# Seven half-width products in place of eight: the w_out product of an mLSTM cell with a gated feed-forward block

## The chip, the cores and the metric

The kernel runs on one core of one Trainium2 chip. The metric is the device time of one execution in microseconds; lower is better. All arithmetic is in fp32.

A core has five engines with a queue of instructions each. TensorE (PE in the profile) multiplies matrices and writes to PSUM, an accumulator memory of eight banks. Its weight loads (PEld), which bring in the stationary operand, overlap its matmuls. VectorE (DVE), ScalarE (ACT) and GpSimd (POOL) work element by element; SyncE (SP) issues transfers. GpSimd does not read or write PSUM in this kernel.

## The reference, cut to what matters

```python
# first part: mLSTM cell over B, H, S, D = 4, 8, 768, 40, step by step over t
m_new  = maximum(f[t] + m, i[t])
C      = exp(f[t] + m - m_new) * C + exp(i[t] - m_new) * outer(v[t], k[t])
n      = exp(f[t] + m - m_new) * n + exp(i[t] - m_new) * k[t]
y[t]   = sigmoid(o[t]) * (C @ q[t]) / maximum(abs(n . q[t]), 1)

# second part: x = y as (B*S, H*D) = (3072, 320)
h   = x @ w_in           # w_in: 320 x 2048
g   = h * cos(h)
out = g @ w_out          # w_out: 2048 x 320
```

The change concerns the last line.

## The kernel before, in words

The sequence of 768 tokens is cut into 6 chunks of 128 (`c`). In each, the cell of every batch `b` (4 of them) is computed with matrices over the 128 tokens: scores, a decay matrix `E`, values, a state carried from chunk to chunk, and a normalisation that writes the transposed input `xT[c]` of the second part. The cell of chunk `c + 1` is computed while the second part of chunk `c` runs. The cells of the first chunk come ahead of everything, in `first_cells`, and the last chunk has no cell beside it.

The second part of a chunk works on 512 tokens at once, the 128 of all four batches. The 2048 hidden columns are 16 blocks of 128, taken in pairs; the pair's number is `f2`, 0 to 7, and `e`, 0 or 1, is the block in the pair. For each pair:

- `Up(c, f2)` computes `h` transposed for the two blocks, each 128 x 512, in two PSUM banks (`pup`, L613 and L616).
- `near`, `rest`, `sin` and `gate` compute the gated value: ScalarE finds the nearest whole number of turns (L621), VectorE takes the rest (L624), ScalarE the sine (L629), and VectorE multiplies (L633). The result is `g`, 128 hidden columns by 512 tokens, in SBUF, in a pool of six buffers.
- `down(c, f2)` adds to the four accumulators `po[c]`, one bank for each batch, 128 tokens x 320 columns, over all 16 blocks. The stationary operand of each matmul is the part of `g` that belongs to a batch; the moving operand is a block of `w_out` (L645). So a pair takes 8 matmuls of 320 columns. After the last pair of a chunk each accumulator is copied by ScalarE (L648) and sent out (L649).

The order of all instructions is written out by hand in `first_cells` and `both_parts`, under `manual_schedule`. One call of `both_parts(c, b)` is a step with two half steps, pairs `2 b` and `2 b + 1`. Each begins with an `Up`, and a `down` follows one half step later: the `down` of a pair comes after the next pair's `Up`, so that ScalarE and VectorE compute `g` in between. The last `down` of a chunk therefore lies in the first half step of the next chunk:

```python
        if f2 > 0:
            down(c, f2 - 1)
        elif c > 0:
            down(c - 1, NF // 2 - 1)
```

Between them lie the cell's parts: `scores` (L445) in the first half step after `Up`, then `weigh` (L451, VectorE), `decay_exponents` of the next cell (L370 on VectorE, L371 on GpSimd) and `decay` (L379, the exponential on ScalarE). After `down` come `values_turned` (L482, L488, into the banks `hp`) and `normalize_turned` (L502 to L514, VectorE, which reads `hp`). The second half step has `seam` (L580, matmuls for the state, into banks of the same pool as `hp`), `state` (L596, VectorE), `weigh_k` (L392, GpSimd), and `turn_blocks` (L410 to L417, VectorE) for the next cell. `fade` (L565) scales the state, on GpSimd in chunk 1 and on VectorE later.

PSUM is fully used: two banks for `pup`, two for the cell (pool `ps_a`), four for `po` (pool `ps_o`).

The weights come in as 64-bit numbers. They are staged in SBUF (`bits`), and turned into fp32 by ScalarE, VectorE and GpSimd (`parts` and `join`, L138 to L149) during chunk 0, pair by pair of blocks for `w_out`.

Of the kernel before, what the change touches and what calls it, by code (L numbers as in the profile page):

```python
# [11 lines left out]
FP = mybir.dt.float32  # L12
# [4 lines left out]
OP = mybir.AluOpType  # L17
# [12 lines left out]
def kernel(  # L30
# [20 lines left out]
    nc = tc.nc  # L51

    B, H, S, D = q.shape
    C = 128
    NC = S // C
# [3 lines left out]
    DM = H * D  # L59
    DFF = moe_w_in.shape[1]  # L60
    NF = DFF // 128
# [13 lines left out]
    p2 = ctx.enter_context(tc.tile_pool(name="p2", bufs=2))  # L75
    p3 = ctx.enter_context(tc.tile_pool(name="p3", bufs=3))
    p4 = ctx.enter_context(tc.tile_pool(name="p4", bufs=4))
    pb = ctx.enter_context(tc.tile_pool(name="pb", bufs=5))
    pc = ctx.enter_context(tc.tile_pool(name="pc", bufs=3))
# [3 lines left out]
    ps_o = ctx.enter_context(tc.tile_pool(name="ps_o", bufs=4, space=bass.MemoryType.PSUM))  # L83
# [15 lines left out]
    p1 = ctx.enter_context(tc.tile_pool(name="p1", bufs=1))  # L99
# [20 lines left out]
    w_out_sb = wp.tile([128, NF, DM], FP, name="w_out_sb")  # L120
# [11 lines left out]
    def parts(dst, bits):  # L132
        n = dst.shape[1]
        hi, lo = bits[:, 0:n, 1], bits[:, 0:n, 0].bitcast(U32)
        t = p2.tile([128, WQ], I32, name="wt", tag="wt")[:, 0:n]
        m = p2.tile([128, WQ], I32, name="wm", tag="wm")[:, 0:n]

        nc.scalar.activation(out=t.bitcast(FP), in_=hi.bitcast(FP), func=AF.Abs)  # L138

        nc.scalar.activation(out=m, in_=lo, func=AF.Copy, scale=2.0 ** -29)  # L140
        return dst, hi, t, m

    def join(dst, hi, t, m, last=None):
        nc.vector.tensor_scalar(out=t.bitcast(FP), in0=t.bitcast(FP), scalar1=LEAST, scalar2=GREATEST,
                                op0=OP.max, op1=OP.min)
        nc.vector.tensor_scalar(out=t, in0=t, scalar1=5, scalar2=2, op0=OP.logical_shift_left,
                                op1=OP.logical_shift_right)
        nc.vector.scalar_tensor_tensor(out=t, in0=hi, scalar=TOP2, in1=t, op0=OP.bitwise_and, op1=OP.bitwise_or)
        (last or nc.gpsimd).tensor_tensor(out=dst.bitcast(I32), in0=t, in1=m, op=OP.add)  # L149
# [210 lines left out]
    def psum_o():  # L360
        return ps_o.tile([128, HP, C], FP, name="pm", tag="o")

    def cols(n, j, width):
        c, b = divmod(n, B)
        return tab[:, c, j, ts(b, H)].unsqueeze(2).to_broadcast([128, H, width])
# [23 lines left out]
    def weigh_k(n):  # L389
        if n < N - B:  # L390
            kw = p2.tile([128, H, D], FP, name="kw", tag="kw")
            nc.gpsimd.tensor_tensor(out=kw, in0=ks[n % NB][:, :, 0:D], in1=cols(n, 1, D), op=OP.mult)  # L392
            kws[n] = kw
# [44 lines left out]
    def scores(n):  # L438
        pool, tag = psum(n)
        qT, kT = qkT[n]  # L440
        ps = [pool.tile([128, HP, C], FP, name="ps", tag=tag) for _ in range(2)]
        for p in range(HP):
            for j in range(2):
                r = slice(64 * j, 64 * j + (64 if n < TURNED else D))
                nc.tensor.matmul(ps[j][:, p], kT[r, p], qT[r, p], start=True, stop=True)  # L445
        pss[n] = ps
# [6 lines left out]
    def values_kept(n):  # L453

        pool, tag = (ps_o, "o") if n == B else psum(n)
        heads_of[n] = None
        if n >= B:
            pq = pool.tile([128, H, D1], FP, name="pq", tag=tag)
            for p in range(HP):
                nc.tensor.matmul(pq[:, 2 * p:2 * p + 2].rearrange("p j d -> p (j d)"), qkT[n][0][:, p],  # L460
                                 st[n % B][:, p].rearrange("p j d -> p (j d)"), start=True, stop=True)
            heads_of[n] = pq
# [136 lines left out]
    gs, po = {}, {}  # L599

    class Up:
# [21 lines left out]
        def rest(self, e):  # L623
            nc.vector.scalar_tensor_tensor(out=self.n[e].bitcast(FP), in0=self.pu[e], scalar=0.25, in1=self.n[e],  # L624
                                           op0=OP.add, op1=OP.subtract)
# [5 lines left out]
        def gate(self, e):  # L631
# [2 lines left out]
                                           op0=OP.mult, op1=OP.mult)  # L634
            gs[self.c, 2 * self.f2 + e] = g

    def down(c, f2):
        if f2 == 0:
            po[c] = [ps_o.tile([128, DM], FP, name="po", tag="o") for _ in range(B)]

        order = [(f, b) for f in (2 * f2, 2 * f2 + 1) for b in range(B)]
        if f2 == NF // 2 - 1:
            order.sort(key=lambda fb: fb[1])
        for f, b in order:
            nc.tensor.matmul(po[c][b], gs[c, f][:, ts(b, C)], w_out_sb[:, f], start=(f == 0), stop=(f == NF - 1))  # L645
            if f == NF - 1:
                o = p2.tile([128, DM], FP, name="o_sb", tag="o_sb")
                nc.scalar.copy(out=o, in_=po[c][b])  # L648
                nc.sync.dma_start(out=out[b * S + c * C:b * S + (c + 1) * C], in_=o)  # L649


    pw, pmu = (ps_u.tile([128, HP, C], FP, name=name, tag="up") for name in ("pw", "pmu"))
# [1 line left out]
    def warm(k, bank=None):  # L654

        for _ in range(k):
            nc.tensor.matmul(bank or pw, nil, nil.unsqueeze(1).to_broadcast([128, HP, 128]), start=True, stop=True)
# [131 lines left out]
    def both_parts(c, b):  # L789

        n = (c + 1) * B + b
        cell = n < N
        begin = c == b == 0
        more = cell and n + 1 < N
        f2 = 2 * b
        up = Up(c, f2)
        if cell:  # L800
            scores(n)
            if begin:
                values_kept(n)

                warm(6, psum_o())
        for e in range(2):
            up.near(e)
        if begin:
            weigh(n)
        for e in range(2):  # L810
            up.rest(e)
        if cell and not begin:
            weigh(n)
        if begin or more and c > 0:
            decay_exponents(n + 1)
        for e in range(2):
            up.sin(e)
            up.gate(e)
        if c == 0 and b == 1:
            sigmoid(1, slice(1, B))  # L820
        if b == B - 1 and c + 2 < NC:
            sigmoid(c + 2)
        h = ()
        if begin:
            h = out_parts()
            w = parts(*pieces.pop(0))
        else:
            if c == 0:
                out_join(*out_parts())
            if pieces:  # L830
                join(*parts(*pieces.pop(0)))
        if begin or more and c > 0:
            decay(n + 1)
        elif more:
            decay_by_bias(n + 1)
        if f2 > 0:
            down(c, f2 - 1)
        elif c > 0:
            down(c - 1, NF // 2 - 1)
        if cell:  # L840
            if n + 2 < N:
                load(n + 2)
            if n < TURNED:
                if not begin:
                    values_kept(n)
                values(n)
                normalize(n)
            else:
                values_turned(n)
            if begin:  # L850
                out_join(*h, nc.vector)
            if TURNED <= n + 2 < N:
                load_G(n + 2)
            if n + 3 < N:
                load_E(n + 3)
            if b == B - 2 and c + 2 < NC:
                load_o(c + 2)
            if n >= TURNED:
                normalize_turned(n)
            fade(n)  # L860
        h = w if begin else ()
        if not begin:
            sin_next()
        if pieces and not begin:
            h = parts(*pieces.pop(0))
        up = Up(c, f2 + 1)
        if cell:
            seam(n)
        for e in range(2):
            up.near(e)  # L870
        for e in range(2):
            up.rest(e)
        if cell and n < TURNED:
            seam_out(n)
        if h:
            join(*h)
        if cell:
            state(n)
        for e in range(2):
            up.sin(e)  # L880
            up.gate(e)
        if more:
            weigh_k(n + 1)
        if pieces:
            join(*parts(*pieces.pop(0)))
        down(c, f2)
        if pieces:
            join(*parts(*pieces.pop(0)))
        if c == 0:
            if b + 2 < B:  # L890
                pieces.extend(weights_in(b + 2))
            h = out_parts()
        if more and n + 1 < TURNED:
            turn(n + 1)
            turn_out(n + 1, c > 0)
        elif more:
            turn_blocks(n + 1)
        if c == 0:
            out_join(*h)

    pieces, outs = [], []
    with tc.manual_schedule():
        first_cells()
        for c in range(NC):
            for b in range(B):
                both_parts(c, b)
        down(NC - 1, NF // 2 - 1)


# [28 lines left out]
```

## Time and profile before

| | |
|---|---|
| time, median of 3 runs | 550.35 us (550.14 to 550.5) |
| span in the profile | 549.5 us |
| granted TensorE clock, mean | 0.993 |
| matmuls of L645 (w_out) | 768 records, 219.3 us busy |
| matmuls of L613 and L616 (w_in) | 384 and 192 records, 175.5 and 54.2 us busy |
| chunk 0's second part begins | 38.7 us |
| chunks 1 to 5 begin | 132.6, 217.2, 301.7, 386.2, 469.0 us |
| last `Up` ends, about | 536.6 us |

Busy time is the union of the records' spans, so that overlapping matmuls are not counted twice; the mean duration of one record is longer than the distance to the next. One fp32 matmul of the code gives two records on PE and two on PEld. "Idle before" is the time in which an engine stood still ahead of a group, and the name behind it is what ended the wait.

### The profile page before, as it was taken

Reading aid. Unit: us, or ns where it says so; the run is one execution under the profiler, and the core shown is the slowest. Engines: PE = TensorE matmul, PEld = TensorE weight load, DVE = VectorE, ACT = ScalarE, POOL = GpSimd, SP = SyncE. Lnnn points to the kernel's source line nnn. Section 1 sums busy time; section 2 is a strip of 40 time slices with the busy share of each in tenths; the row PEclk is TensorE's granted clock in tenths of the full one; section 3 lists DMA queues with packets and bytes.
Section 4 is the critical chain, followed back from the end, with each engine's and each line's share of the span. In section 5 each row is a group of like instructions: output and inputs, shape, how many; then the busy total and the mean of one; then the engine's idle time right before and its main releaser. Section 6 shows DMA issues by size and latency. Waiting matters only on the chain.

```text
span 549.5 us, 9153 instructions
## 1 busy us (share of the span) xinstructions
PE 538.8 (98%) x3395; PEld 317.4 (58%) x3395; DVE 355.9 (65%) x692; ACT 264.4 (48%) x420; POOL 76.7 (14%) x112
## 2 busy tenths in 40 slices
PE   9989899999999999999999999999999999999997
PEld 6865566665565565565565555555655655555554
DVE  5876987968777677677667667667666665232311
ACT  4868795775632544543435344427335323331312
POOL 5531433523110100101101101100000000000000
PEclk9979999999999999999999999999999999999999
DMA  9999985851265651166625076635075000100001
GB/s 143 206 226 221 239 220 145 189 124 33 77 142 129 148 124 36 50 136 138 151 75 107 26 158 139 143 78 110 4 173 109 8 14 12 51 1 1 0 0 50
DMA packets 134509, 56.83 MB, mean 103 GB/s; under 512 B 72080, under 2 KB 130528, under 8 KB 134464
## 3 DMA queue, kind: packets, MB, share of 16 engines
q1 hardware_dynamic: 134320, 56.04, 46.0%
q8 instruction: 27, 0.44, 0.3%
q0 software_dynamic: 96, 0.18, 0.2%
q14 instruction: 18, 0.15, 0.1%
q10 hardware_dynamic: 48, 0.02, 0.0%
HBM read 50.00 MB, written 6.21 MB: 102 GB/s over the span
## 4 chain that ended last, share of the span: by engine, by line
PE 85%; DVE 5%; DMA 4%; SPq 3%; POOL 1%; ACT 1%; issue 1%; DVEq 0%; ACTq 0%; POOLq 0%
PE po L645 37%; PE pup L613 28%; PE pup L616 8%; PE hp L488 3%; PE ps L445 3%; PE hp L482 2%; PE pu L580 1%; DMA E<-M_d 1%; SPq L327 1%; PE pt L426 1%; SPq L129 1%; DMA qs<-in_q_dram 1%; DMA bits<-in_moe_w_out_dram 1%; DMA M_d<-M_rows 1%; DMA bits<-in_moe_w_in_dram 1%
## 5 line engine op out<-in xcount | busy, mean ns | idle before, releaser
L645 PE MATMUL po<-w_out_sb,g 128*128 128x320 f32 x768 | 219.3, 439 | 1.3 <-POOL w_out_sb L149 1.0
L645 PEld LDWEIGHTS po<-w_out_sb,g 128*128 128x128 f32 x768 | 142.0, 190 | 67.0 <-issue 8.3
L613 PE MATMUL pup<-xT,w_in_sb 128*128 128x512 f32 x384 | 175.5, 599 | 0.9 <-POOL w_in_sb L149 0.6
L621 ACT ACTIVATE n<-pup 128x512 int32<-128x512 f32 x96 | 52.0, 593 | 214.3 <-PE pup L616 214.3
L624 DVE SCALAR_TENSOR_TENSOR n<-pup,n 128x512 f32<-128x512 f32 x96 | 61.9, 686 | 135.1 <-ACT n L621 135.0
L613 PEld LDWEIGHTS pup<-xT,w_in_sb 128*128 128x128 f32 x384 | 71.2, 191 | 77.6 <-issue 63.9
L629 ACT ACTIVATE n<-n 128x512 f32<-128x512 f32 x96 | 58.8, 630 | 12.1 <-DVE n L624 12.1
L633 DVE SCALAR_TENSOR_TENSOR g<-pup,n 128x512 f32<-128x512 f32 x96 | 61.7, 685 | 1.7
L371 POOL TENSOR_SCALAR_AFFINE_SELECT E<-E 128x1024 f32<-128x1024 f32 x19 | 20.8, 1094 | 292.9 <-DVE E L370 273.6
L616 PE MATMUL pup<-xT,w_in_l 64*128 64x512 f32 x192 | 54.2, 641 | 0.0
L616 PEld LDWEIGHTS pup<-xT,w_in_l 64*128 64x128 f32 x192 | 14.4, 184 | 36.4 <-issue 35.6
L451 DVE TENSOR_TENSOR E<-ps,E 128x512 f32<-128x512 f32 x48 | 30.7, 680 | 6.1 <-PE ps L445 6.1
L379 ACT ACTIVATE E<-E 128x1024 f32<-128x1024 f32 x21 | 22.2, 1058 | 21.7 <-POOL E L371 17.2
L410 DVE STREAM_TRANSPOSE t<-qs 128x512 f32<-128x512 f32 x32 | 32.3, 1087 | 0.0
L445 PEld LDWEIGHTS ps<-t,t 40*128 40x128 f32 (+1 forms) x384 | 25.1, 188 | 9.7 <-issue 8.9
L445 PE MATMUL ps<-t,t 40*128 40x128 f32 (+1 forms) x384 | 25.8, 274 | 0.0
L370 DVE TENSOR_TENSOR E<-E,tab 128x1024 f32<-128x1024 f32 x19 | 23.1, 1216 | 0.4 <-DMA E<-M_d 0.4
L379 ACT ACT_TABLE_LOAD x18 | 23.1, 1283 | 0.3
L778 ACT ACT_TABLE_LOAD x18 | 23.1, 1283 | 0.3
L502 DVE STREAM_TRANSPOSE room<-hp 128x128 f32<-128x128 f32 x32 | 8.6, 306 | 22.5 <-PE hp L488 22.5
L488 PE MATMUL hp<-E,vs 128*32 128x128 f32 x512 | 17.3, 276 | 0.0
L417 DVE STREAM_TRANSPOSE room<-o 128x256 f32<-128x256 f32 x32 | 17.2, 618 | 0.0
(128 smaller groups left out, 428.9 us busy)
## 6 DMA issues: line engine op xcount, KB each, us to landing
E<-M_d SPq DMA_DIRECT2D x22, 512.0 KB
bits<-in_moe_w_in_dram SPq DMA_DIRECT2D x40, 128.0 KB
bits<-in_moe_w_out_dram SPq DMA_DIRECT2D x8, 640.0 KB
room<-G_d SPq DMA_DIRECT2D x32, 128.0 KB
ks<-in_k_dram SPq DMA_DIRECT2D x24, 160.0 KB
vs<-in_v_dram SPq DMA_DIRECT2D x24, 160.0 KB
out_dram<-o_sb SPq DMA_DIRECT2D x24, 160.0 KB
qs<-in_q_dram SPq DMA_DIRECT2D x32, 80.0 KB
```

The source lines that it names most:

```text
L379: nc.scalar.activation(out=Es[n], in_=Es[n], func=AF.Exp, scale=-1.0)
L410: nc.vector.transpose(out=dst.rearrange("r p (t x) -> r p x t", x=T4), in_=src.rearrange("r p (x d) -> r p x d", x=T4)[:, :, :, 0:32])
L445: nc.tensor.matmul(ps[j][:, p], kT[r, p], qT[r, p], start=True, stop=True)
L451: nc.vector.tensor_tensor(out=w, in0=pss[n][j], in1=w, op=OP.mult)
L488: nc.tensor.matmul(hps[n][j][ts(p, 32), half], vs[n % NB][:, h, lo:lo + DA], Es[n][:, h], start=False, stop=True, skip_group_check=True)
L613: nc.tensor.matmul(pu, w_in_sb[:, i, ts(block(f2, e), 128)], x(i), start=(i == 0), stop=False)
L616: nc.tensor.matmul(pu, w_in_l[r, f2], x(NK, r), start=False, stop=True)
L621: nc.scalar.activation(out=self.n[e], in_=self.pu[e], func=AF.Copy, bias=0.25)
L624: nc.vector.scalar_tensor_tensor(out=self.n[e].bitcast(FP), in0=self.pu[e], scalar=0.25, in1=self.n[e], op0=OP.add, op1=OP.subtract)
L629: nc.scalar.activation(out=r, in_=r, func=AF.Sin, scale=TWO_PI_DOWN)
L633: nc.vector.scalar_tensor_tensor(out=g, in0=self.pu[e], scalar=TWO_PI, in1=self.n[e].bitcast(FP), op0=OP.mult, op1=OP.mult)
L645: nc.tensor.matmul(po[c][b], gs[c, f][:, ts(b, C)], w_out_sb[:, f], start=(f == 0), stop=(f == NF - 1))
```

## The change

Write the 128-token parts of `g` for batches 0 and 1 and the two blocks of a pair as a 2 x 2 matrix of blocks, A11 (batch 0, block 0), A21 (batch 1, block 0), A12 and A22, and the two halves of 160 columns of the two blocks of `w_out` as B11, B12 (block 0) and B21, B22 (block 1). The product of two such matrices needs eight block products. Winograd's form of Strassen's algorithm needs seven, with sums formed before and after:

| sums of g (`S`) | differences of w_out (`T`) | products |
|---|---|---|
| S0 = A21 + A22 | T0 = B12 - B11 | P1 = A11 B11, P2 = A12 B21 |
| S1 = S0 - A11 | T1 = B22 - T0 | P3 = S3 B22, P4 = A22 T3 |
| S2 = A11 - A21 | T2 = B22 - B12 | P5 = S0 T0 |
| S3 = A12 - S1 | T3 = T1 - B21 | P6 = S1 T1, P7 = S2 T2 |

The outputs are C11 = P1 + P2, C12 = P1 + P6 + P5 + P3, C21 = P1 + P6 + P7 - P4 and C22 = P1 + P6 + P7 + P5. Each of the seven is summed over the eight pairs in PSUM, so that the last sums are formed once for each chunk.

The change does this for batches 0 and 1 in chunks 1 to 5. Batches 2 and 3, and all of chunk 0, keep their products. The parts:

- GpSimd forms the `T` of a pair once (`two_differences`, in the last half step of chunk 0 and three of chunk 1), in buffers that held the staged weights. It forms the `S` of every pair and chunk after the second `gate` (`sums`).
- The accumulators are grouped by bank: P1, P2, P6 in the first, P5, P3, P4 in the second, batch 2 and P7 in the third, batch 3 in the fourth. Only the first matmul into a bank clears it.
- At a chunk's end ScalarE copies P1, VectorE makes seven additions out of PSUM, and ScalarE copies batches 3 and 2. ScalarE's copies stand behind all writes to their bank. The last `down` of a chunk is now issued ahead of `decay`, and its copies and transfers (`rest`) after it. At the very end of the kernel, the seven products come before the two whole batches.

```diff
+    def differences(p, T):
+        B11, B12, B21, B22 = (w_out_sb[:, 2 * p + e, ts(h, DH)] for e in range(2) for h in range(2))
+        for i, (x, y) in enumerate(((B12, B11), (B22, T[:, 0]), (B22, B12), (T[:, 1], B21))):
+            nc.gpsimd.tensor_tensor(out=T[:, i], in0=x, in1=y, op=OP.subtract)
...
+    def sums(c, f2):
...
+        S = p2.tile([128, 4, C], FP, name="sg", tag="wt")
+        A11, A21, A12, A22 = (gs[c, 2 * f2 + e][:, ts(b, C)] for e in range(2) for b in range(2))
+        for i, (x, y, op) in enumerate(((A21, A22, OP.add), (S[:, 0], A11, OP.subtract),
+                                        (A11, A21, OP.subtract), (A12, S[:, 1], OP.subtract))):
+            nc.gpsimd.tensor_tensor(out=S[:, i], in0=x, in1=y, op=op)
...
+    def down_parted(c, f2):
...
+            po[c] = [ps_o.tile([128, 3 * DH + 32], FP, name="po", tag="o") for _ in range(4)]
+        P1, P2, P6, P5, P3, P4 = (po[c][i // 3][:, ts(i % 3, DH)] for i in range(6))
+        P7 = po[c][2][:, DM:DM + DH]
...
+        very_end = end and c == NC - 1
+        if not very_end:
+            for b in range(2, B):
+                whole(b)
+        product(P1, g0[:, 0:C], w0[:, lo], True)
+        product(P2, g1[:, 0:C], w1[:, lo])
+        product(P6, S[:, 1], T[:, 1])
+        product(P7, S[:, 2], T[:, 2])
+        product(P5, S[:, 0], T[:, 0], True)
+        product(P3, S[:, 3], w1[:, hi])
+        product(P4, g1[:, C:2 * C], T[:, 3])
...
+        nc.scalar.copy(out=U[:, 0], in_=P1)
+        for dst, x, y, op in ((o2[:, 0, lo], U[:, 0], P2, OP.add), (U[:, 0], U[:, 0], P6, OP.add),
+                              (U[:, 1], U[:, 0], P7, OP.add), (U[:, 0], U[:, 0], P5, OP.add),
+                              (o2[:, 0, hi], U[:, 0], P3, OP.add), (o2[:, 1, lo], U[:, 1], P4, OP.subtract),
+                              (o2[:, 1, hi], U[:, 1], P5, OP.add)):
+            nc.vector.tensor_tensor(out=dst, in0=x, in1=y, op=op)
+        if very_end:
+            for b in (3, 2):
+                whole(b)
...
     def down(c, f2):
+        if parted(c):
+            return down_parted(c, f2)
...
             up.gate(e)
+        sums(c, f2)
...
+        rest = None
+        if b == 0 and c > 0 and parted(c - 1):
+            rest = down(c - 1, NF // 2 - 1)
         if begin or more and c > 0:
             decay(n + 1)
...
+        elif rest:
+            rest()
         elif c > 0:
             down(c - 1, NF // 2 - 1)
...
+        sums(c, f2 + 1)
         if more:
             weigh_k(n + 1)
+        if c == 0 and b == B - 1 or c == 1 and b < B - 1:
+            two_differences(c * (2 * b + 2))
```

In the changed kernel the products of both kinds stand in line 689, the sums of `g` in line 672, the weight differences in line 651, the copy of P1 in line 715 and the seven additions in line 720.

More of the change, by code (lines that the diff above doesn't have):

```diff
@@ L635, in gate, with parted, two_differences @@
             gs[self.c, 2 * self.f2 + e] = g
+    DH = DM // 2
+    Ts, sg = {}, {}
+    def parted(c):
+        return c > 0
+    def differences(p, T):
+        B11, B12, B21, B22 = (w_out_sb[:, 2 * p + e, ts(h, DH)] for e in range(2) for h in range(2))
+        for i, (x, y) in enumerate(((B12, B11), (B22, T[:, 0]), (B22, B12), (T[:, 1], B21))):
+            nc.gpsimd.tensor_tensor(out=T[:, i], in0=x, in1=y, op=OP.subtract)
+        Ts[p] = T
+    def two_differences(p):
+        if p < 6:
+            T = pc.tile([128, 2, 4, DH], FP, name="T", tag="bits")
+            for e in range(2):
+                differences(p + e, T[:, e])
+        else:
+            for e in range(2):
+                differences(p + e, pb.tile([128, 4, DH], FP, name="T", tag="bits"))
@@ new lines, in sums @@
+    def sums(c, f2):
+        if not parted(c):
+            return
+        S = p2.tile([128, 4, C], FP, name="sg", tag="wt")
[3 more added lines that the diff above has]
+            nc.gpsimd.tensor_tensor(out=S[:, i], in0=x, in1=y, op=op)
+        sg[c, f2] = S
@@ new lines, in down_parted, with product, whole, whole_out @@
+    def down_parted(c, f2):
+        end = f2 == NF // 2 - 1
+        if f2 == 0:
+            po[c] = [ps_o.tile([128, 3 * DH + 32], FP, name="po", tag="o") for _ in range(4)]
+        P1, P2, P6, P5, P3, P4 = (po[c][i // 3][:, ts(i % 3, DH)] for i in range(6))
+        P7 = po[c][2][:, DM:DM + DH]
+        g0, g1 = (gs[c, 2 * f2 + e] for e in range(2))
+        w0, w1 = (w_out_sb[:, 2 * f2 + e] for e in range(2))
+        S, T = sg[c, f2], Ts[f2]
+        lo, hi = slice(0, DH), slice(DH, DM)
+        def product(out, g, w, first=False):
+            nc.tensor.matmul(out, g, w, start=(f2 == 0 and first), stop=end, skip_group_check=True)
+        def whole(b):
+            for e, (g, w) in enumerate(((g0, w0), (g1, w1))):
+                product(po[c][b][:, 0:DM], g[:, ts(b, C)], w, e == 0)
+        def whole_out(b):
+            o = p2.tile([128, DM], FP, name="o_sb", tag="o_sb")
+            nc.scalar.copy(out=o, in_=po[c][b][:, 0:DM])
+            result(c, b, o)
+        very_end = end and c == NC - 1
[9 more added lines that the diff above has]
+        product(P4, g1[:, C:2 * C], T[:, 3])
+        if not end:
+            return None
+        o2 = p2.tile([128, 2, DM], FP, name="o2", tag="wm")
+        U = p1.tile([128, 2, DH], FP, name="hs", tag="hs")
+        nc.scalar.copy(out=U[:, 0], in_=P1)
[7 more added lines that the diff above has]
+                whole(b)
+        def rest():
+            for b in range(2):
+                result(c, b, o2[:, b])
+            for b in (3, 2):
+                whole_out(b)
+        return rest
@@ L637, in down, with result @@
+    def result(c, b, o):
+        nc.sync.dma_start(out=out[b * S + c * C:b * S + (c + 1) * C], in_=o)
     def down(c, f2):
+        if parted(c):
+            return down_parted(c, f2)
         if f2 == 0:
@@ L648, in down @@
                 nc.scalar.copy(out=o, in_=po[c][b])
-                nc.sync.dma_start(out=out[b * S + c * C:b * S + (c + 1) * C], in_=o)
+                result(c, b, o)
     pw, pmu = (ps_u.tile([128, HP, C], FP, name=name, tag="up") for name in ("pw", "pmu"))
@@ L906 @@
                 both_parts(c, b)
-        down(NC - 1, NF // 2 - 1)
+        down(NC - 1, NF // 2 - 1)()
 _INS = ['q', 'k', 'v', 'i_gate', 'f_gate', 'o_gate', 'moe_w_in', 'moe_w_out']
```

## The prediction, made before the changed kernel ran

> **What bounds the kernel now.** I read the page's busy shares first, then the slices by stage, then the chain of work that ended last, then the groups by line with their shapes kept apart, then the timeline around one half step. The first three say the same thing.
>
> ```profile
> PE 538.8 (98%) x3395; PEld 317.4 (58%) x3395; DVE 355.9 (65%) x692; ACT 264.4 (48%) x420; POOL 76.7 (14%) x112
> ...
> PE 85%; DVE 5%; DMA 4%; SPq 3%; POOL 1%; ACT 1%; issue 1%; DVEq 0%; ACTq 0%; POOLq 0%
> ```
>
> ```profile
> 217.20:301.70 84.50, 84.50 (x609) 48.53 (x608) 59.48 (x122) 37.86 (x54) 7.18 (x9) 1.00 0.48 107
> 301.70:386.20 84.50, 84.50 (x609) 48.53 (x608) 59.50 (x121) 37.69 (x54) 6.48 (x8) 1.00 0.47 107
> 386.20:469.00 82.80, 82.80 (x546) 46.99 (x545) 53.09 (x103) 31.56 (x49) 3.28 (x3) 1.00 0.24 54
> 469.00:536.60 67.60, 67.60 (x210) 35.12 (x208) 18.05 (x28) 18.05 (x36) 0.00 (x0) 1.00 0.03 10
> ```
>
> The columns of the second fence are stretch, length, then busy time of PE, PEld, DVE, ACT and POOL, the granted clock and DMA. From 132.6 us, where chunk 1 begins, PE never stops: in chunks 2 to 5 its busy time equals the stretch, and the chain in chunk 2 consists of PE alone. A saved nanosecond of PE is therefore a saved nanosecond of kernel until another engine falls behind. GpSimd is almost idle.
>
> A busy PE is not yet a PE at its limit, so I take the cost of one matmul from its spacing:
>
> ```profile
> 128.23 4.57 PE L645 MATMUL po<-w_out_sb,g 128*128 128x320 f32 x16
> ```
>
> ```profile
> L470 PE MATMUL ph<-vs,E 128*128 128x41 f32 x128 | 15.5, 282 | 0.2 <-DVE E L451 0.2
> L470 PEld LDWEIGHTS ph<-vs,E 128*128 128x128 f32 x128 | 15.0, 192 | 0.7 <-DVE E L451 0.4
> ```
>
> One `down` is 8 matmuls in the code and 16 in the trace, since each fp32 matmul appears as two with a weight load each. Of the 4.57 us the last takes 0.43 and the first costs about 0.10 more than its successors (its start follows another tile shape), so the spacing is (4.57 - 0.43 - 0.10) / 15 = 269 ns, which is also the start-to-start time of the single records. The durations of 439 ns overlap. The rows of L470 give the other limit: its matmuls have 41 columns, so the weight load of 128 columns must set their pace. Loads last 192 ns each but 128 of them cover 15.0 us, 117 ns each with the ends of 8 bursts; start to start the records show 112 ns.
>
> [...]
>
> **The change part by part.**
> *The products.* In chunks 1 to 5, 8 half steps each, two of four batches lose 4 matmuls of 320 columns and get 7 of 160; 40 such exchanges. Removed: 4 x 2 x 269 = 2152 ns. Added: 7 x 2 x the spacing at 160 columns. No row has this width with full 128 x 128 weights. Bounds: the weight-load pace, 112 ns (L470 at 41 columns and L357 at 128 columns both run at it)[...]. The larger must hold; I take 136. The load is hidden with 24 ns to spare. 14 x 135.8 = 1901 ns. Saving 252 ns an exchange, x 40 = 10.1 us.
>
> *Sums on GpSimd* (L672 of the changed kernel, four 128 x 128 operations a half step). Two-input rows: 723 ns for 320 elements (L392), 501 for 164 (L565 on POOL). The line through them gives 450 ns at 128[...]. Four take about 1.8 us, 2.0 at most. They start at the end of the second `gate` and are needed by the third product of a `down` that comes after the next `Up`. In chunk 3, gates end at 311.90 and 322.03, the `down`s that use them start at 318.43 and 328.31, and the third product comes 1.7 us later: 8.0 us or more. The work of PE itself hides them. Behind them in GpSimd's queue stand `weigh_k` (its product is wanted a half step later), the mask L371 of the following step (which waits for VectorE until 331.90), and in chunk 1 `fade`. Only after the last `Up` is there no next one to hide behind; there P6 and P3 may wait some tenths of a us.
>
> *Weight differences on GpSimd*: 32 operations of 160 columns, about 0.5 us each, in four lots of 4 us in chunk 0's last half step and chunk 1's. GpSimd is busy 8.7 of 84.6 us in chunk 1: hidden. They overlap VectorE's L413 (two SBUF inputs, 0.68 us), whose result has 2 us to spare.
>
> *More readers and waits.* A `gate` now also waits for GpSimd's reading of a `g` three `Up`s old; that is long over. From the last gate to the next `Up` there are at least 0.81 us of slack in chunks 1 to 4 (322.03 to 322.84 is the shortest), and the second bank is needed 0.86 later still. The shorter `down` takes 0.25 from it. PE gets three satisfied GpSimd waits a half step. L470 has two such waits a burst and keeps its 112 ns, so I cost them at nothing; the other end is 50 ns each (the length of a wait record on PEld) less the 24 to spare, 26 x 3 x 40 = 3.1 us.
>
> *The end of a chunk.* Four copies of 0.43 us on ScalarE become one of half width and two whole ones; VectorE gets seven adds of 160 columns, at 0.32 (L596, 164 columns) 2.2 us in a chain. What is queued behind them is `normalize_turned`, whose reading of `hp` frees the banks that `seam` needs. In chunk 3 VectorE ends its gates at 311.90 and would wait for `hp` until 313.22. With the adds it starts at 314.15, 0.93 later, and ends with `hp` (L511) at 316.4 instead of 315.5. PE reaches L580 at 317.99, or 317.7 after the change. Hidden by `Up`, with 1.3 us to spare. ScalarE's first copy waits for P6, at about 310.7, and holds back the exponential by 0.2 us, which serves the next step. The accumulators are free by about 314.7; the next first `down` starts at 318. ScalarE's 10.4 us of waiting for output buffers mostly goes, but was off the path.
>
> *The very end.* Products come first, then the two whole batches, so that VectorE adds beside PE. The last copy is still 0.43 us after the last matmul, and the final transfer is the same: no change beyond the saving already counted.
>
> Sum: 550.35 - 10.1 = 540.3 us.
>
> **The rivals.**
> *Weight loads bind.* If a load could not start until the one before had finished, half-width products would go at 190 ns: 14 x 190 = 2660, 508 more than before, x 40 = 20.3, so 570.7 us, slower. For it: LDWEIGHTS lasts 190 ns, longer than 136. Against it: L470 and L357.
> *GpSimd becomes the bound.* If one 128-column sum took over 2.0 us, four would exceed the 8.0 us given, with a stall in all 40: at 2.5 us each, 2.0 x 40 - 10 = +70, so 620 us, slower. Against it: the three GpSimd rows, all below 1.6 us for up to 640 elements.
> *Small waits give part back.* Waits at their upper price (3.1 us), adds that cost 0.55 us each so that L580 waits 0.3 us four times (1.2), and 0.7 at the end: up to 5 us back, 541.5 to 545.3. For it: three GpSimd waits in a stream with only 24 ns to spare.
> *Hidden anyway.* PE's saving only uncovers another engine, about 550. Against it: the slack of 0.8 us and more in each half step against 0.25 taken.
>
> **How the numbers follow.** 0.72 for the forecast, 0.18 for small waits (still faster), 0.08 for the two slow rivals, 0.02 for hidden. So faster 0.90, same 0.02, slower 0.08. The range goes from 539.2 (a little more at the end and at the chunk boundaries than counted) to 544.5, most of the small-waits case.
>
> **What would show it.** The L689 rows should split into 320-column matmuls at 269 ns and 560 records of 160 columns at 136 ns start to start; the 84.5 us of chunks 2 and 3 should become 82.5 with PE still busy throughout; GpSimd should rise by 80 to 100 us with no PE idle time against it. It is wrong if half-width products are spaced at 140 ns or more, if PE waits on `sg`, or if L580 or the first whole product of a chunk waits for VectorE or ScalarE.

## The result and the profile after

The changed kernel takes 541.09 us (540.97 to 541.97), against 550.25 for the kernel before in the same measurement: a ratio of 0.9838, 95% interval 0.9821 to 0.9855, or 8.0 to 9.9 us. The prediction was 540.3 in a range of 539.2 to 544.5.

The busy shares and the chain of the page after, to be held beside those of before:

```profile
PE 529.1 (98%) x3635; PEld 334.4 (62%) x3635; DVE 368.6 (68%) x727; ACT 262.1 (49%) x415; POOL 166.9 (31%) x304
...
PE 85%; DVE 4%; SPq 4%; DMA 4%; POOL 1%; ACT 1%; issue 1%; DVEq 0%; POOLq 0%
```

PE has 240 records more and is busy 9.7 us less; GpSimd has 90 us more. The chain is still PE's. The same kernel by stage, from the first matmul of each chunk to that of the next (stretch, length, busy time of PE, PEld, DVE, ACT, POOL, clock, DMA share and GB/s):

```profile
132.59:215.38 82.79, 82.79 (x651) 51.52 (x650) 61.10 (x123) 37.86 (x54) 33.88 (x62) 1.00 0.48 109
215.38:297.88 82.50, 82.50 (x658) 52.02 (x657) 62.25 (x128) 37.29 (x53) 22.89 (x41) 1.00 0.48 109
297.88:380.38 82.50, 82.50 (x658) 52.02 (x657) 62.27 (x128) 37.29 (x53) 22.89 (x41) 1.00 0.48 109
380.38:461.14 80.76, 80.76 (x594) 50.47 (x593) 55.85 (x110) 31.00 (x48) 17.23 (x35) 1.00 0.23 55
```

Before, chunks 2 and 3 took 84.5 us and chunk 4 82.8. Each has lost 2.0 us, and PE's busy time still fills the stretch: the saving came whole, and no wait took its place. Chunk 1 lost 1.8, since its first half step still holds the last `down` of chunk 0, which is unchanged. The groups of w_out's products, by shape (busy us, mean ns of one, idle us before):

```profile
L689 PE MATMUL po<-w_out_sb,g 128*128 128x320 f32 x320 | 96.7, 445 | 0.0
L689 PE MATMUL po<-T,sg 128*128 128x160 f32 x240 | 39.4, 300 | 0.0
L689 PE MATMUL po<-w_out_sb,g 128*128 128x160 f32 x160 | 28.3, 299 | 0.0
L689 PE MATMUL po<-T,g 128*128 128x160 f32 x80 | 17.4, 299 | 0.0
L689 PE MATMUL po<-w_out_sb,sg 128*128 128x160 f32 x80 | 17.4, 299 | 0.0
```

The last four rows are the 560 half-width records, none with idle time ahead of it. Their mean duration of 300 ns overlaps the next records. Start to start they are 136 ns apart, whether the stationary operand is `g` or a sum from GpSimd. The timeline of one `down` shows it too (its first row merges the 8 whole records with the 4 of P1 and P2):

```profile
241.49 2.96 PE L689 MATMUL po<-w_out_sb,g 128*128 128x320 f32 x12
...
244.29 0.98 PE L689 MATMUL po<-T,sg 128*128 128x160 f32 x6
245.10 0.43 PE L689 MATMUL po<-w_out_sb,sg 128*128 128x160 f32 x2
245.38 0.43 PE L689 MATMUL po<-T,g 128*128 128x160 f32 x2
```

(0.98 - 0.30) / 5 = 136 ns.

### The profile page after: what moved, and what is told of

The parts are those of the page before. It is cut to its first block, busy times and chain, and to the rows that moved or that the text cites. A ratio compares the mean times of both kernels' runs of the same rounds, so it can differ in the third digit from the quotient of the medians.

```text
span 539.1 us, 9945 instructions
## 1 busy us (share of the span) xinstructions
PE 529.1 (98%) x3635; PEld 334.4 (62%) x3635; DVE 368.6 (68%) x727; ACT 262.1 (49%) x415; POOL 166.9 (31%) x304
## 4 chain that ended last, share of the span: by engine, by line
PE 85%; DVE 4%; SPq 4%; DMA 4%; POOL 1%; ACT 1%; issue 1%; DVEq 0%; POOLq 0%
PE po L689 32%; PE pup L613 29%; PE pup L616 9%; PE po L746 4%; PE hp L488 3%; PE ps L445 3%; PE hp L482 2%; SPq L129 1%; PE pu L580 1%; DMA bits<-in_moe_w_in_dram 1%; DMA o<-in_o_gate_dram 1%; SPq L327 1%; DMA qs<-in_q_dram 1%; DVE wt L146 1%; PE pt L426 1%; DMA M_d<-M_rows 1%
## 5 line engine op out<-in xcount | busy, mean ns | idle before, releaser
L689 PE MATMUL po<-w_out_sb,g 128*128 128x320 f32 (+1 forms) x480 | 118.6, 396 | 0.0
L613 PEld LDWEIGHTS pup<-xT,w_in_sb 128*128 128x128 f32 x384 | 70.0, 191 | 73.9 <-issue 61.9
L689 PEld LDWEIGHTS po<-w_out_sb,g 128*128 128x128 f32 x480 | 83.5, 190 | 36.7 <-issue 9.1
L672 POOL TENSOR_TENSOR sg<-g 128x128 f32<-128x128 f32 x80 | 36.6, 457 | 192.7 <-DVE g L633 191.2
L616 PE MATMUL pup<-xT,w_in_l 64*128 64x512 f32 x192 | 54.2, 641 | 0.0
L689 PE MATMUL po<-T,sg 128*128 128x160 f32 x240 | 39.4, 300 | 0.0
L746 PE MATMUL po<-w_out_sb,g 128*128 128x320 f32 x128 | 36.6, 439 | 1.3 <-POOL w_out_sb L149 1.0
L616 PEld LDWEIGHTS pup<-xT,w_in_l 64*128 64x128 f32 x192 | 14.4, 184 | 36.4 <-issue 35.6
L689 PEld LDWEIGHTS po<-T,sg 128*128 128x128 f32 x240 | 34.8, 190 | 0.2
L410 DVE STREAM_TRANSPOSE t<-qs 128x512 f32<-128x512 f32 x32 | 32.8, 1101 | 0.0
L746 PEld LDWEIGHTS po<-w_out_sb,g 128*128 128x128 f32 x128 | 23.7, 190 | 11.0 <-POOL w_out_sb L149 1.3
```

Source lines behind the costliest of these rows:

```text
L410: nc.vector.transpose(out=dst.rearrange("r p (t x) -> r p x t", x=T4), in_=src.rearrange("r p (x d) -> r p x d", x=T4)[:, :, :, 0:32])
L613: nc.tensor.matmul(pu, w_in_sb[:, i, ts(block(f2, e), 128)], x(i), start=(i == 0), stop=False)
L616: nc.tensor.matmul(pu, w_in_l[r, f2], x(NK, r), start=False, stop=True)
L672: nc.gpsimd.tensor_tensor(out=S[:, i], in0=x, in1=y, op=op)
L689: nc.tensor.matmul(out, g, w, start=(f2 == 0 and first), stop=end, skip_group_check=True)
```

## The experiments

Times of whole runs of one kernel scatter by about 1 us in either direction. Most of that lies ahead of chunk 1, which begins between 131.35 and 133.06 us in the ten profiles, although the code up to there is nearly the same. It goes with the granted TensorE clock: every profile shows a half clock somewhere between 21 and 41 us, for 3.41 us in all in three of them, where chunk 1 begins at 131.35 to 131.73, and for 6.83 us in the other seven, where it begins at 131.91 to 133.06. So the last column gives the profiled time from the first matmul of chunk 1 to the end, which repeats to 0.02 us (the changed kernel and its repetition below).

| run | us | ratio to before, 95% interval | from chunk 1 on, us |
|---|---|---|---|
| before | 550.25 | 1 | 416.84 |
| changed | 541.09 | 0.9838 (0.9821 to 0.9855) | 406.52 |
| e0_changed_again | 541.47 | 0.9828 (0.9800 to 0.9856) | 406.51 |
| e1_eight_halves | 552.05 | 1.0017 (1.0004 to 1.0030) | 417.59 |
| e2_narrow_products | 529.22 | 0.9611 (0.9592 to 0.9631) | 394.74 |
| e3_sums_thrice | 539.88 | 0.9808 (0.9792 to 0.9824) | 406.50 |
| e4_adds_thrice | 555.65 | 1.0090 (1.0057 to 1.0124) | 422.05 |
| e5_after_decay | 540.67 | 0.9818 (0.9794 to 0.9842) | 406.50 |
| e6_adds_twice | 541.82 | 0.9838 (0.9816 to 0.9859) | 408.31 |
| i1_last_chunk_both | 539.11 | 0.9796 (0.9775 to 0.9816) | 405.07 |

The kernel before, measured beside the later runs, had medians of 550.79 (e0, e1, e2, i1) and 550.32 (e3 to e6).

### The changed kernel again

> The changed kernel once more, with more rounds. If the whole gain is the spacing of the matmuls (40 x 252 ns = 10.1 us), the ratio to before is 0.9816 and the time about 540.2; the first measurement, 0.9838, was then low by chance. If something outside the profiled span gives a microsecond back, the ratio stays near 0.984 while the span is shorter by over 10 us.

The interval holds both values and so tells nothing between them. The trace does: the stretch from chunk 1 on is 10.3 us shorter than before in both profiles. The measured medians differ by 9.2 and 9.3, about 1 us less. The clock of each run, which is on record for this measurement, accounts for most of that: the median before is a run with a mean clock of 0.997, the changed median lies between two runs at 0.994. The runs at 1.000 took 548.99 and 549.26 us before and 538.85 after, 10.1 and 10.4 apart; those at 0.993 and 0.994 have medians of 551.46 and 541.64, 9.8 apart. At like clocks the gain is about 10 us. The code ahead of chunk 1 is the same but for the weight differences, which GpSimd makes in the last half step, and no profile shows them to cost time.

### Does the width set the pace, or the weight load?

The first run keeps eight products, but half as wide:

```diff
-            nc.tensor.matmul(po[c][b], gs[c, f][:, ts(b, C)], w_out_sb[:, f], start=(f == 0), stop=(f == NF - 1))
+            for h in range(2) if c > 0 and b < 2 else ():
+                nc.tensor.matmul(po[c][b][:, ts(h, DM // 2)], gs[c, f][:, ts(b, C)], w_out_sb[:, f, ts(h, DM // 2)],
+                                 start=(f == 0 and h == 0), stop=(f == NF - 1), skip_group_check=True)
+            if c == 0 or b > 1:
+                nc.tensor.matmul(po[c][b], gs[c, f][:, ts(b, C)], w_out_sb[:, f], start=(f == 0), stop=(f == NF - 1))
```

> The kernel before, with each matmul of batches 0 and 1 in chunks 1 to 5 cut into two of 160 columns: eight half-width products, no sums, no GpSimd work. Theory (columns set the pace, the weight load is hidden): 16 x 135.8 against 8 x 269 ns, 21 ns more in each of 40 half steps, so 0.8 us more than before, about 551. Rival (a load of 190 ns binds): 16 x 190 = 3040, 888 more, x 40 = 35.5 us, about 586.

From chunk 1 on it takes 417.59 - 416.84 = 0.75 us more, with 0.8 expected. Twice as many matmuls and weight loads of half the width cost 19 ns a half step. The rival that had loads of 190 ns in line is gone. So the gain of the change is the one product of eight that is left out, 2 x 136 ns a half step, less those 19 to 21 ns.

The second run asks where that ends. It leaves part of the sums out, so it doesn't compute the output:

```diff
+            if f2 > 0 and w.shape[-1] == DH:
+                out, w = out[:, 0:96], w[:, 0:96]
             nc.tensor.matmul(out, g, w, start=(f2 == 0 and first), stop=end, skip_group_check=True)
```

> The changed kernel with its seven products cut to 96 columns in all pairs but the first of a chunk; the other 64 columns are left out. Theory (the larger of columns and weight load): spacing 112 ns, not 82.5; 14 x (135.8 - 112) = 333 ns less in 35 half steps, 11.7 us, so about 529.4. If columns alone count: 14 x 53.3 = 746 ns x 35 = 26 us, about 515.

It takes 11.8 us less than the changed kernel, with 11.7 expected. The timeline of a `down` (the first row is merged as above):

```profile
238.33 2.84 PE L691 MATMUL po<-w_out_sb,g 128*128 128x320 f32 x12
241.00 0.83 PE L691 MATMUL po<-T,sg 128*128 128x96 f32 x6
241.67 0.39 PE L691 MATMUL po<-w_out_sb,sg 128*128 128x96 f32 x2
241.90 0.39 PE L691 MATMUL po<-T,g 128*128 128x96 f32 x2
```

(0.83 - 0.28) / 5 = 110 ns; start to start nearly all the records are 110 to 112 ns apart, not the 82.5 forecast for columns alone (an estimate, about what the line through 136 ns at 160 columns and 269 at 320 gives). That is the pace of L470, 112 ns, whose products have 41 columns and weights of the same size, so the columns don't set it. It is not a fixed cost of every record either: the 16 records of L580, with 41 columns and weights of 40 columns, start within 0.31 us in the changed kernel. What is left of the three is the load of the 128 x 128 weights; no run varied it alone. Half-width products of 160 columns, at 136 ns, stand 24 ns above that floor.

### Does GpSimd's work cost anything?

```diff
-        for i, (x, y, op) in enumerate(...):
-            nc.gpsimd.tensor_tensor(out=S[:, i], in0=x, in1=y, op=op)
+        for _ in range(1 if (c, f2) == (NC - 1, NF // 2 - 1) else 3):
+            for i, (x, y, op) in enumerate(...):
+                nc.gpsimd.tensor_tensor(out=S[:, i], in0=x, in1=y, op=op)
```

> The changed kernel with each of the GpSimd sums of g made three times over (the last pair's once): 3.7 us more GpSimd work in 39 half steps, 143 us in all. Theory (the sums have over 7 us before their product is due): no PE wait, 541, within 0.2%. Rival (GpSimd near its limit, or its reads slow VectorE's chain onto the path): a stall in most half steps, 5 us or more.

PE doesn't notice: chunks 2 and 3 take 82.50 us to the hundredth.

```profile
214.13:296.63 82.50, 82.50 (x658) 52.02 (x657) 66.28 (x128) 37.30 (x53) 51.15 (x105) 1.00 0.49 110
```

GpSimd is busy 51.15 us instead of 22.89. VectorE, with the same 128 instructions, is busy 66.28 instead of 62.25. It is slowed, but within its slack. One group shows how; first the changed kernel, then this run (duration min/median/max):

```profile
L514 DVE TENSOR_TENSOR xT<-room,room x16: 417/418/419, 146.8 to 454.9; 128x256 f32<-128x256 f32 x16
```

```profile
L514 DVE TENSOR_TENSOR xT<-room,room x16: 670/671/675, 145.9 to 454.0; 128x256 f32<-128x256 f32 x16
```

L514 reads two operands from SBUF. L511, with the same shape and one operand in PSUM, stays at 395 ns in both. Why the two engines slow each other is not shown by these runs. GpSimd pays too: in this run a sum beside L514 takes 633 ns instead of 455, while those wholly beside L410 or L417, transposes with one operand, keep 453 to 464.

### How much room do the seven additions have?

Before the seven additions, 14 (then 7) more of the same size were put in, in chunks 1 to 4:

```diff
+        for _ in range(0 if very_end else 14):
+            nc.vector.tensor_tensor(out=o2[:, 0, lo], in0=U[:, 0], in1=P2, op=OP.add)
```

> The changed kernel with 14 more VectorE additions of 160 columns ahead of the seven at the end of chunks 1 to 4, some 4.2 us. The trace of the changed kernel leaves 1.4 us between the release of hp and L580. Theory (the seven fit into a spare time of 1.4 us and no more): L580 waits about 2.8 us in chunks 2 and 3, and in chunk 4, which has no L580, the next Up waits some 2 us for a late gate; 7.8 us in all (5.6 to 9), about 549. Rival (VectorE is off the path there): 541.

The wait is there, but the cost is 15.5 us from chunk 1 on instead of 7.8. In chunk 2 of this run:

```profile
225.18 4.92 DVE L717 TENSOR_TENSOR o<-hs,po 128x160 f32<-128x160 f32 x14
...
234.47 0.78 PE L580 MATMUL pu<-vs,kw 128*40 128x41 f32 x16 [3.29 <-DVE room L511]
235.17 1.44 PE L689 MATMUL po<-w_out_sb,g 128*128 128x320 f32 x2
```

The additions took 0.35 us each, not 0.30. L580 starts 3.36 us late (3.88 after the start of the last L616 record instead of 0.52). The matmuls behind it are then 533 ns apart instead of 269. The view by stretches shows why, in the clock behind POOL's busy time (1.00, then 0.55):

```profile
226.00:233.00 7.00, 5.17 (x32) 1.95 (x20) 6.28 (x22) 2.51 (x5) 1.23 (x3) 1.00 0.01 4
233.00:240.00 7.00, 5.54 (x26) 3.92 (x27) 6.74 (x17) 2.38 (x5) 0.52 (x2) 0.55 0.64 180
```

By the trace's clock records the granted clock was halved at 233.75, when PE had stood still for 2.6 us of these 3.3, and stayed so for 6.83 us. That cost another 2.9 us. So 6.3 in chunk 2, and as much in chunk 3. Chunk 4, with no L580, lost 2.8 to a late gate, where 2 were expected:

```profile
415.47 1.98 PE L613 MATMUL pup<-xT,w_in_sb 128*128 128x512 f32 x4 [2.49 <-DVE g L633]
```

This wait of 2.49 us left the clock at 1.00. The other three runs of e4 have no trace; the four took 553.4, 555.3, 556.1 and 557.9 us at mean clocks of 0.991, 0.985, 0.982 and 0.978, so the loss to the clock is not the same each time.

> As the run with 14 more additions, but with 7 more, 2.46 us at the 0.35 us each that were measured there. Theory (a spare time of 1.4 to 1.5 us, and the halved TensorE clock in that run came from PE standing still for 3.3 us): L580 waits 1.0 us in chunks 2 and 3, a late gate holds the next Up of chunk 4 for 0.2, 2.2 us in all, and the granted clock stays full from chunk 1 on: about 543. Rival (the clock drops after any wait of this kind): 2.8 us more in each of chunks 2 and 3, about 549.

L580 starts 0.89 us late in chunk 2 and 0.90 in chunk 3 (1.41 and 1.42 after the start of the last L616 record instead of 0.52). The first of them:

```profile
232.10 0.71 DVE L511 TENSOR_TENSOR room<-room,hp 128x256 f32<-128x256 f32 x2
...
232.63 0.51 PE L580 MATMUL pu<-vs,kw 128*40 128x41 f32 x16 [0.82 <-DVE room L511]
```

The clock stays at 1.00. From chunk 1 on the run takes 1.8 us more than the changed kernel, with 2.2 expected: the late gate of chunk 4 cost nothing to speak of (chunk 4 is 0.03 longer), and chunks 2 and 3 are 0.9 longer each. 2.46 us more of additions and 0.89 of lateness put the spare time at 1.6 us. Both runs agree (4.92 - 3.36 = 1.6). The 1.4 us of the forecasts run to the end of the second of the two L511 operations, which each read one bank of `hp`. But L580 needs one bank, and starts 0.15 us after the first L511 in both runs, before the second has ended. In the changed kernel the first L511 ends at 312.18 and L580 starts at 313.92, 1.6 us later than it could. The seven additions fit; one more such chain would not.

### The place of the last down

```diff
-        if b == 0 and c > 0 and parted(c - 1):
-            rest = down(c - 1, NF // 2 - 1)
         if begin or more and c > 0:
             decay(n + 1)
         elif more:
             decay_by_bias(n + 1)
+        if b == 0 and c > 0 and parted(c - 1):
+            rest = down(c - 1, NF // 2 - 1)
```

> The changed kernel with the last down of a chunk issued after decay again, as before the change: the copy of P1 then stands behind the exponential on ScalarE. Theory: the additions start 1.6 us later, 0.2 more than the spare time, and L580 waits 0.2 to 0.3 us in chunks 2 and 3: 0.5 us in all, 541.6. If the order were of no use: no wait at L580. If ScalarE's queue is what matters more: a wait of over 1 us in each chunk.

There is no wait: 406.50 us from chunk 1 on, the same as the changed kernel. The forecast of 0.5 us failed. At the end of chunk 2's work, in chunk 3 of this run, the first of the two L511 operations, then both merged, then L580:

```profile
312.34 0.38 DVE L511 TENSOR_TENSOR room<-room,hp 128x256 f32<-128x256 f32 x1
...
312.34 0.71 DVE L511 TENSOR_TENSOR room<-room,hp 128x256 f32<-128x256 f32 x2
...
313.05 0.51 PE L580 MATMUL pu<-vs,kw 128*40 128x41 f32 x16
```

The additions start 1.4 us later, not 1.6; why the 0.2 are missing was not followed up. The spare time is 1.6 us, not 1.4. So 0.2 are left: the first bank of `hp` is read by 312.73, and L580 starts at 313.05, 0.52 after the start of the last L616 record, as in the changed kernel. The new place costs and gains nothing by itself; it keeps those 1.4 us spare.

### Seven products for all four batches, where PSUM allows it

Two sets of seven accumulators of 160 columns need 2240 columns; the four tiles of `po`, 3 x 160 + 32 = 512 columns each, have 2048. In the last chunk no cell is computed, and the two banks of `ps_a` are free:

```diff
+        if c == NC - 1 and f2 < LAST:
+            S = p4.tile([128, 4, C], FP, name="sgb", tag="E")
...
+    def down_last(c, f2):
...
+            po[c] += [ps_a.tile([128, 3 * DH + 32], FP, name="pob", tag="a") for _ in range(2)]
...
+        seven(first, sg[c, f2], T, g0, g1, w0, w1, 0, f2, end, (0, 3, 4))
+        if f2 < LAST:
+            seven(second, sgb[f2], T, g0, g1, w0, w1, 2, f2, f2 == LAST - 1, (0, 3, 4))
+            if f2 == LAST - 1:
+                kept[c] = p2.tile([128, 2, DM], FP, name="o2", tag="wm")
+                seven_out(second, kept[c])
+            return None
```

Here LAST is 6. Pairs 6 and 7 of batches 2 and 3 go as whole products into the two banks of `po` that also hold one half-width accumulator each, and are added to `kept` at the end, so that the second set of additions is out of the way of the last one.

> The changed kernel, with seven products for batches 2 and 3 as well in pairs 0 to 5 of the last chunk, where the cell's two PSUM banks are free. Theory: 6 x 252 ns less, 1.5 us below the changed kernel, with the end as before. Rival (twice the sums on GpSimd and seven more additions on VectorE come onto the path in the last chunk): PE waits on sgb or on a gate in the last chunk and the time is not below the changed kernel's.

From the first `Up` of the last chunk to its last, the changed kernel and this one:

```profile
461.14:522.35 61.21, 61.21 (x240) 36.11 (x239) 20.11 (x35) 17.61 (x35) 12.12 (x28) 1.00 0.03 12
```

```profile
461.50:521.20 59.70, 59.70 (x276) 38.41 (x275) 20.46 (x37) 17.91 (x36) 22.04 (x52) 1.00 0.03 12
```

1.51 us less, as expected, and 1.45 with the end. The ratio to before is 0.9796, the lowest of all runs that compute the whole output. In time alone its interval overlaps that of the changed kernel's repetition in the same measurement; the difference of 1.5 us rests on the profiles.

## Why the prediction was right

*PE alone is the path from chunk 1 on.* Shown: every saved matmul came off the span, in the changed kernel, in the narrow products and in the last chunk.

*The spacing at 160 columns.* Predicted as 135.8 ns, measured as 136, and 252 ns a half step as 251 (84.51 - 82.50 = 2.01 us for eight). The figure for the columns follows from the profile before. There the records of 512 columns, of 0.59 us each, start (3.60 - 0.59) / 7 = 0.43 us apart, 429 ns record by record:

```profile
301.71 3.60 PE L613 MATMUL pup<-xT,w_in_sb 128*128 128x512 f32 x8
```

Those of 320 columns start 269 ns apart, and the line through the two gives 135.7 ns at 160 (an estimate). That the larger of this and of the 112 ns of the weight load holds was the author's assumption; measured were 136 ns at 160 columns (the changed kernel) and 110 to 112 at 96 (e2). The 190 ns of a weight load are a duration, and their spacing is 112; e1 and e2 settle this.

*The satisfied waits for GpSimd* cost nothing, as taken: the products with `sg` are 136 ns apart like the others.

*The sums* were predicted at 450 ns and measured at 457, the differences at 500 and measured at 524. The second sum, the first that a product needs, ended at least 6.9 us before P6 in all pairs but the last. That PE hides them is shown, but the 8.0 us from gate to P6 were right by luck. P6 starts 2.8 us into a `down`, not 1.7, as the two whole batches come first; so chunk 3 has 8.9 us or more. The least is in chunk 5, where no cell fills the half step and which the prediction didn't read: there it is 8.0. The price of the slow rival was too high, since it let all four sums come before P6, which needs two. And `fade` on GpSimd ends ahead of chunk 1, so it never stood behind the sums. In the last pair P6 and P7 wait for their sums:

```profile
531.65 1.22 PE L689 MATMUL po<-T,sg 128*128 128x160 f32 x6
```

This is 0.98 in other pairs; the 0.24 are the tenths that were foreseen.

*The chunk's end.* The additions were put at 2.2 us and took 2.33; the spare time at L580 was put at 1.3, counted from the second L511, and is 1.6 from the first, by the trace and by loading it.

*What was not foreseen.* `weigh_k` (L392) rose from 723 to 971 ns in the mean, as it now stands behind the sums and runs while VectorE's L413 reads two SBUF operands (1.17 us each from chunk 1 on). Nothing waits for it. And the stretch from the start of the last `Up` of the kernel to the end is 0.77 us shorter (17.52 to 16.75), where 0.50 was counted. PE saves only 0.26 of these 0.50, as the last pair waits for its sums. The other 0.52 lies behind the last matmul (4.06 to 3.54), where the prediction saw no change. The last copy starts 0.03 us after that matmul instead of 0.21, for which it had waited for an output buffer by the profile. The other 0.34 lies between the last copy and the end; the run with the old order (e1) has neither gain, and the cause of the 0.34 was not tried.

*The sum.* 10.1 us were predicted, 10.3 are in the trace. The measured 9.2 is lower, most likely by the clock ahead of chunk 1: in the repetition, runs of like clock lie 9.8 to 10.4 apart. In the first measurement the clocks of the kernel before are not on record.

## What to carry to other kernels

Where TensorE is the path, price a matmul by the distance from start to start, and not by the duration of either record; here that distance was the larger of what the columns took (136 ns at 160, 269 at 320) and what the weight load took (110 to 112 ns, with products of 96 and of 41 columns). Then count how many columns each product may lose before the load sets the pace: seven half-width products pay here since 160 columns lie above the floor; with halves of 96, 14 x 112 = 1568 ns would stand against 8 x 162.5 = 1300 for whole products of 192 columns, a loss (an estimate: 162.5 lies on the line through 136 ns at 160 columns and 269 at 320). Put the extra additions on engines whose results are due a half step later, and test the room that they have by multiplying them, since a wait of 0.8 us cost 0.9 us and one of 2.5 us cost 2.8, but one of 3.3 us cost 6.3, with the clock halved.

## What the runs showed of the hardware

- In the middle of a busy stretch TensorE stood still for 3.3 us and was given half the clock from 2.6 us into the wait, for 6.83 us (e4). Waits of 2.5 us (e4, chunk 4) and 0.8 us (e6) left it at full. In the profiles before and after, the clock changes at points that lie whole multiples of 3.413 us apart: 6.83 and 508.59 us (2 and 149 times) before, 6.83 and 498.35 us (2 and 146 times) after. The wait in e4 had lasted less than one such step, the 2.6 us, when the clock was halved. In e1 the clock was halved at 22.01 with PE busy for 3.00 of the 3.41 us before (below), so with no wait of more than 0.41 us in them. What counts as busy for the clock is not shown by these runs.

```profile
18.60:22.01 3.41, 3.00 (x38) 2.65 (x37) 2.22 (x4) 2.11 (x6) 1.44 (x3) 1.00 0.78 219
```

- A VectorE operation with two SBUF operands and a GpSimd operation with two slowed each other, not evenly: L514 went from 418 to 671 ns and the sum beside it from 455 to 633 (e3), but L392 from 723 to 1170 while L413 beside it went only from about 680 to 710. With one operand in PSUM, L511 kept its 395 ns.
